# Gate and value products of four column tiles as seven block products, in a chain of attention and two feed-forwards

## The chip, the cores and the metric

One core of one Trainium2 chip runs the whole kernel. The metric is the device time of an execution in microseconds (us): 484.2 us before the change, the median of 3 runs (484.12 to 484.35). Engines: TensorE (PE in the profile, PEld its weight loads), VectorE (DVE), ScalarE (ACT), GpSimd (POOL) and SyncE (SP), which issues the DMAs here.

## The reference, cut to what matters

Attention over 2 x 12 heads, 448 tokens and 64 columns with capped scores, then two feed-forwards over the 896 tokens. The change is in the second one, and in five small instructions at the start:

```
scores = cap * tanh(scale * q @ k.T / cap)          # attention, 12 heads x 2
x  = moe(x, w_in, w_out, g_ln)                      # first feed-forward: 896 x 768 out
g  = x @ w_gate                                     # 896x768 @ 768x1536
silu = g * (1 / (1 + exp(-g)))
val  = x @ w_val                                    # 896x768 @ 768x1536
out  = (silu * val) @ w_out                         # 896x1536 @ 1536x768
```

The weights arrive as 64-bit floats and are brought to 32 bits on the chip.

## The kernel before, in words

Every 32-bit operand of a product is split into a high and a low part (`split`, L627: the high part is a ScalarE copy, the low part a VectorE subtraction), and `mm3` (L175) issues three matmuls for one product: high by high, high by low, low by high. Accumulators are PSUM tiles of one bank; eight banks are handed round under the tag `m`.

The stage of gate and value (loop at L947) goes over `K2` = 12 column tiles `fc` of 128 columns (the third to sixth are `fc` 2 to 5, called tile 2 to tile 5 here), and in each over the tokens in two blocks, 384 and 512. `ff2_gv` (L603) makes `g` and then `v` for a block: 6 row tiles of `x2` times three matmuls, so 18 matmuls for one accumulator. ScalarE takes the Silu of `g` into `ee`, VectorE multiplies by `v`, forms sums for the output stage (`S1f`, `S3f`) and splits the result into `a`. So a column tile is 72 matmuls, 36 of 384 and 36 of 512 tokens.

`load_gv` (L593) brings the weights of tile `fc + 1` while tile `fc` runs: one DMA of 766 KB into one of two `raw` buffers, `f32_shifted` (L158: two ScalarE passes and one VectorE pass into one of two `f32` buffers), and a split into `g4`, of which there are four, two for even and two for odd tiles. `load_w2` (L632) does the same for a tile of the output weights; L954 calls it once in each of tiles 2 to 8.

The matrix `x2` (tokens after the first feed-forward, transposed) is made just before by `ff1_x2` (L570): each block of 24 matmuls is drained as a ScalarE copy (high) and a VectorE subtraction (low). At the same time `load_w_out` (L558) makes the next weights with both engines.

The order is set by a scheduler within this stage (`in_order` off): it places instructions by its own model of their times, under the waits that the tiles require. Each engine then runs its own list strictly in that order, and an instruction that waits holds up all behind it.

In `setup` (L190), L201 to L206 convert -9 * 2^30 to a 32-bit integer and back, and add what it differs from -2^31 to `cap`; `c1`, the scale of the first tanh, is made from that.

Of the kernel before, what the change touches and what calls it, by code (L numbers as in the profile page):

```python
# [37 lines left out]
class Kernel:  # L38
# [135 lines left out]

    def mm3(self, out, lhsT, rhs, start, stop):  # L175

        mm = self.PE.matmul
        mm(out, lhsT[0], rhs[0], start=start, stop=False)
        mm(out, lhsT[0], rhs[1], start=False, stop=False)
        mm(out, lhsT[1], rhs[0], start=False, stop=stop)  # L180

# [8 lines left out]
    def setup(self):  # L190
# [9 lines left out]
        nc.gpsimd.dma_start(cp, self.cap.to_broadcast([128, 1]))  # L200
        low, least = cs[:, 6:7], cs[:, 7:8]  # L201
        self.G.memset(low, -9.0 * 2.0 ** 30)
        self.A.activation(least.bitcast(I32), low, AF.Copy)
        self.V.tensor_copy(low, least.bitcast(I32))
        self.V.tensor_scalar(low, low, 2.0 ** 31, None, op0=ALU.add)
        self.V.tensor_tensor(cp, cp, low, op=ALU.add)  # L206
        self.V.reciprocal(c1, cp)
# [362 lines left out]
    def ff1_x2(self, j, get, N, o):  # L570
# [3 lines left out]
        def part(a, z):  # L574
            def f():
# [17 lines left out]
    def load_gv(self, fc, i):  # L593

        if i == 0:
            self.gvs[fc] = [self.g4[(fc % 2) * 2 + n].rearrange("p (u k f) -> p u k f", u=2, f=128) for n in range(2)]
# [6 lines left out]
    def ff2_gv(self, fc, N, o):  # L603
# [236 lines left out]
    def run(self):  # L840
# [69 lines left out]
        self.g4 = [p.tile([128, 1536], F32R, name=f"g4_{i}", tag=f"g4_{i}") for i, p in enumerate((wb, wb, gb, gb))]  # L910
        w8 = self.w8 = wb.tile([128, 8, 2, n], F32R, name="w8", tag="w8")
        X = self.slot("x", [128, KD, 2, 896], "x2")
# [19 lines left out]
        big = self.big = self.slot("l", [128, 6144], "a_0")  # L932
        self.A12t, self.A22t = (ap.tile([128, KD, 2, w], F32R, name=f"a_{i}", tag=f"a_{i}") for i, w in ((1, n), (2, 512)))
        self.S1f, self.S3f = (ap.tile([128, KD, n], F32, name=f"s_{i}", tag=f"s_{i}") for i in (1, 3))
        w1 = ap.tile([128, 2, n], F32R, name="w1", tag="w1")
        t1 = ap.tile([128, n], F32, name="t1", tag="t1")
# [64 lines left out]
```

## Time and profile before

| | before |
|---|---|
| median of 3 runs | 484.20 us |
| the profiled execution's own time | 485.15 us |
| its span in the profile | 483.4 us |
| PE busy | 478.9 us, 99% of the span |
| DVE busy | 337.8 us, 70% |
| ACT busy | 290.3 us, 60% |
| POOL busy | 20.9 us, 4% |
| granted TensorE clock | 1.00 of full speed, 2.4 GHz |

The span is what the profiler saw of the engines; the own time of the same execution is 1.75 us more, and lies 0.95 us over the median of the runs. Matmuls are pipelined: the mean of a matmul's record is longer than the distance from one to the next, which is read from the chain of waits or from busy time over count. Idle time of an engine that nobody waits for costs nothing.

### The profile page before, as it was taken

What the parts mean: (1) busy time and instruction counts of PE and PEld (TensorE: products, weight loads), DVE (VectorE), ACT (ScalarE), POOL (GpSimd) and SP (SyncE); (2) the same over time, 40 slices, a digit from 0 to 9 for tenths busy, and PEclk for the clock granted to TensorE, in tenths of its full rate; (3) what the DMA queues carried; (4) which work ended last, traced back from release to release, by engine and by line L of the source; (5) the groups of instructions that cost most, each with busy time, mean ns of one, the idle gap of its engine ahead of it and who ended that gap; (6) DMA issues with size and microseconds to landing.
All of it is one profiled execution on the core that took longest, in us unless ns stands there. A gap on an engine that the chain in (4) does not pass through costs nothing.

```text
span 483.4 us, 7642 instructions
## 1 busy us (share of the span) xinstructions
PE 478.9 (99%) x3042; PEld 394.7 (82%) x3042; DVE 337.8 (70%) x577; ACT 290.3 (60%) x407; POOL 20.9 (4%) x63
## 2 busy tenths in 40 slices
PE   9999999999999999999999999999999999999997
PEld 7444444538888899989899988899988899999996
DVE  3689999987769987475546454556554427999991
ACT  5999999931233796457857766667764416335220
POOL 1020101021000010000000000000000000000000
PEclk9999999999999999999999999999999999999999
DMA  6886575002001323236663454654462401010012
GB/s 176 202 190 153 146 185 146 20 2 87 0 1 41 90 75 101 83 113 194 196 196 109 152 187 139 196 184 134 137 194 68 131 0 57 11 60 7 18 54 94
DMA packets 65060, 52.35 MB, mean 108 GB/s; under 512 B 35584, under 2 KB 61952, under 8 KB 64256
## 3 DMA queue, kind: packets, MB, share of 16 engines
q1 hardware_dynamic: 64992, 51.86, 36.0%
q8 instruction: 24, 0.39, 0.3%
q14 instruction: 12, 0.10, 0.1%
q0 software_dynamic: 32, 0.00, 0.0%
HBM read 49.10 MB, written 2.75 MB: 107 GB/s over the span
## 4 chain that ended last, share of the span: by engine, by line
PE 99%; DVE 1%; issue 0%
PE g L30 18%; PE v L30 18%; PE p L30 16%; PE x L30 12%; PE h L30 12%; PE pv L30 8%; PE sc L30 7%; PE S L30 4%; PE lt L30 1%; PE T L30 1%; PE warm L30 1%; DVE ks L30 0%; PE T_q L30 0%; PE warm_T L30 0%; DVE ee L30 0%; PE T_k L30 0%
## 5 line engine op out<-in xcount | busy, mean ns | idle before, releaser
L30 PE MATMUL g<-x,g 128*128 128x512 f32 (+1 forms) x432 | 91.7, 363 | 0.0
L30 PE MATMUL v<-x,g 128*128 128x512 f32 (+1 forms) x432 | 90.8, 362 | 0.0
L30 PEld LDWEIGHTS g<-x,g 128*128 128x128 f32 x432 | 78.5, 188 | 8.9
L30 PEld LDWEIGHTS v<-x,g 128*128 128x128 f32 x432 | 78.2, 188 | 8.6
L30 PE MATMUL h<-wi,x 128*128 128x512 f32 x252 | 59.1, 392 | 0.0
L30 PEld LDWEIGHTS h<-wi,x 128*128 128x128 f32 x252 | 46.8, 188 | 11.2 <-issue 1.5
L30 ACT ACTIVATE P<-sc,consts 112x896 f32<-112x896 f32 x48 | 45.3, 1009 | 3.8 <-PE sc L30 2.2
L30 ACT ACTIVATE P<-P,consts 112x3584 f32<-112x3584 f32 (+1 forms) x13 | 39.7, 3061 | 0.1
L30 PE MATMUL pv<-P,v 112*32 112x448 f32 x384 | 38.5, 540 | 0.0
L30 PEld LDWEIGHTS sc<-ks 64*112 64x112 f32 x288 | 23.3, 171 | 18.3 <-issue 7.7
L30 PE MATMUL sc<-ks 64*112 64x448 f32 x288 | 35.8, 379 | 0.3
L30 PE MATMUL x<-lB,wo 128*128 128x256 f32 (+1 forms) x192 | 35.2, 337 | 0.0
L30 PEld LDWEIGHTS x<-lB,wo 128*128 128x128 f32 x192 | 29.6, 189 | 3.4
L30 PEld LDWEIGHTS pv<-P,v 112*32 112x32 f32 x384 | 12.2, 110 | 23.0 <-issue 20.9
L30 ACT ACTIVATE ee<-h,sms 128x512 f32<-128x512 f32 x14 | 9.5, 683 | 33.2 <-DVE sms L30 33.2
L30 DVE TENSOR_TENSOR g<-wg,g 128x768 fp32r<-128x768 f32 x12 | 11.5, 959 | 25.2 <-ACT g L30 25.2
L30 PE MATMUL x<-lA,wo 128*128 128x384 f32 x144 | 27.4, 338 | 0.0
L30 PE MATMUL p<-w,a 128*128 128x384 f32 x144 | 26.7, 334 | 0.0
L30 PEld LDWEIGHTS x<-lA,wo 128*128 128x128 f32 x144 | 25.2, 188 | 0.5
L30 DVE TENSOR_TENSOR ee<-v,ee 128x384 f32<-128x384 f32 (+2 forms) x24 | 12.5, 520 | 18.5 <-PE v L30 17.7
L30 PEld LDWEIGHTS p<-w,a 128*128 128x128 f32 x144 | 25.2, 188 | 0.1
L30 ACT ACTIVATE g<-wg 128x768 fp32r<-128x768 f32 x12 | 10.1, 846 | 24.0 <-PE g L30 23.3
(178 smaller groups left out, 737.5 us busy)
## 6 DMA issues: line engine op xcount, KB each, us to landing
wg_raw<-in_moe_w_gate_dram SPq DMA_DIRECT2D x12, 765.8 KB, 4.3
wv_raw<-in_moe_w_val_dram SPq DMA_DIRECT2D x12, 765.8 KB, 4.2
wi_raw<-in_moe_w_in_dram SPq DMA_DIRECT2D x6, 1024.0 KB, 6.8
wo_raw<-in_moe_w_out_dram SPq DMA_DIRECT2D x12, 512.0 KB, 3.5
w_raw<-in_moe_w_out_dram SPq DMA_DIRECT2D x6, 767.6 KB, 4.3
v<-in_v_dram SPq DMA_DIRECT2D x24, 112.0 KB, 3.8
kq<-in_k_dram SPq DMA_DIRECT2D x22, 112.0 KB, 2.8
kq<-in_q_dram SPq DMA_DIRECT2D x22, 112.0 KB, 2.7
```

The lines of the kernel that those rows point to most:

```text
L30: i = f(*a, **k)
```

## The change: what it does

For tiles 2 to 5 the products of gate and value are formed together as a 2 x 2 block product: rows gate and value of the weights, their 768 rows in halves of 384, and the tokens in halves of 448. Seven products of sums of blocks (Strassen's scheme in Winograd's form) take the place of eight: each is 3 row tiles times 3 matmuls of 448 tokens, so 63 matmuls for a tile. The sums have to be made:

- of `x2`, once: `ff1_x2` also copies each accumulator to `xf` in 32 bits (one more ScalarE instruction for each of 14 blocks), and `x_sums` makes four differences of 384 x 448 (three row tiles of 448, 1344 elements a partition) and splits them into `T1` to `T4`, in tiles 0 and 1.
- of the weights, for each tile: `sum_steps(fc + 1)` loads and converts both, two sums of 384 elements go to GpSimd (`S`), two to VectorE, and the splits go to `g4[0]` (A11, A12), `g4[1]` or `g4[3]` (S2, S4), `g4[2]` (S3, S1) and `w1` (A22). Only the second of these is double-buffered.
- of the results: accumulators `a` (named `g_` in the rows), `b` and `c` are each used twice: a first product is read out, then a second is added to it in the same bank. `ee` holds `sg`, `c22`, `p1` and `u2` once.

`xf` takes the room of `w8`, so the loads of the output weights move from tiles 2 to 8 to tiles 6 to 9, two in each of tiles 6 to 8. `load_gv` takes tile 6 as before. The conversion at the start (L201 to L206) is left out.

```diff
-        low, least = cs[:, 6:7], cs[:, 7:8]
-        self.G.memset(low, -9.0 * 2.0 ** 30)
-        self.A.activation(least.bitcast(I32), low, AF.Copy)
-        self.V.tensor_copy(low, least.bitcast(I32))
-        self.V.tensor_scalar(low, low, 2.0 ** 31, None, op0=ALU.add)
-        self.V.tensor_tensor(cp, cp, low, op=ALU.add)
...
                     self.hi_act(hi, ps)
                     self.lo_dve(lo, ps, hi)
+                    self.A.activation(self.xf[:, j, o:o + N], ps, AF.Copy)
...
+    def x_sums(self, i):
+        x = [self.xf[:, 3 * (m // 2):3 * (m // 2) + 3, 448 * (m % 2):448 * (m % 2) + 448] for m in range(4)]
+        d, p, m, t = ((0, 1, 0, 0), (1, 3, 1, 2), (3, 3, 0, 1), (2, 2, 3, 3))[i]
+        self.V.tensor_tensor(x[d], x[p], x[m], op=ALU.subtract)
+        self.split([self.T[t][:, u] for u in range(2)], x[d])
+    def sum_steps(self, fc):
+        add, sub = ALU.add, ALU.subtract
+        f = []
+        for n, w in zip("gv", (self.w_gate, self.w_val)):
+            src = w[:, fc * 128:(fc + 1) * 128].rearrange("(k p) f -> p k f", p=128)
+            f.append(self.f32_shifted(self.load_shifted(src, f"w{n}_{fc}"), f"w{n}_{fc}").rearrange("p (h x) -> p h x", h=2))
+        g, v = f
+        s1 = self.t1
+        pair = lambda t: [t.rearrange("p (h u x) -> p h u x", h=2, u=2)[:, :, u] for u in range(2)]
+        t = self.gvs[fc] = [self.g4[0], self.g4[1 + fc % 2 * 2], self.g4[2], self.w1]
+        S = self.G
+        S.tensor_tensor(s1, v[:, 0], v[:, 1], op=add)
+        S.tensor_tensor(v[:, 0], g[:, 0], v[:, 0], op=sub)
+        def first():
+            self.split(pair(t[0]), g)
+            self.V.tensor_tensor(g[:, 0], s1, g[:, 0], op=sub)
+            self.V.tensor_tensor(g[:, 1], g[:, 1], g[:, 0], op=sub)
+            self.split(pair(t[1]), g)
+        def second():
+            hi, lo = pair(t[2])
+            for m, x in enumerate((v[:, 0], s1)):
+                self.split((hi[:, m], lo[:, m]), x)
+        def third():
+            self.split([self.w1[:, u] for u in range(2)], v[:, 1])
+        return first, second, third
+    def ff2_gv_seven(self, fc):
+        V, add, mult = self.V, ALU.add, ALU.mult
+        n, k, ee = self.HN, fc, self.ee
+        a, s24, s31, a22 = self.gvs[fc]
+        half = lambda t, h: t.rearrange("p (h u k f) -> p h u k f", h=2, u=2, k=3)[:, h]
+        A11, A12, S2, S4, S3, S1 = (half(t, h) for t in (a, s24, s31) for h in range(2))
+        A22 = a22.rearrange("p u (k f) -> p u k f", k=3)
+        X = lambda kh, th: [[self.x2[3 * kh + c][:, u, 448 * th:448 * th + 448] for u in range(2)] for c in range(3)]
+        T1, T2, T3, T4 = ([[t[:, u, c] for u in range(2)] for c in range(3)] for t in self.T)
+        bank = lambda m: self.pt.tile([128, 512], F32, name=f"{m}_{fc}", tag="m")[:, :448]
+        def product(acc, w, x, start):
+            for c in range(3):
+                self.mm3(acc, (w[:, 0, c], w[:, 1, c]), x[c], start and c == 0, c == 2, not start)
+        sg, c22, p1, u2 = (ee[:, 448 * m:448 * m + 448] for m in range(4))
+        last = fc + 1 == self.KD
+        first, second, third = (lambda: None,) * 3 if last else self.sum_steps(fc + 1)
+        if last:
+            self.load_gv(fc + 1, 1)
+        a = bank("g")
+        product(a, A11, X(0, 0), True)
+        self.A.activation(p1, a, AF.Copy)
+        b = bank("b")
+        product(b, S2, T2, True)
+        V.tensor_tensor(u2, p1, b, op=add)
+        product(a, A12, X(1, 0), False)
+        self.A.activation(sg, a, AF.Silu)
+        first()
+        if last:
+            self.load_gv(fc + 1, 0)
+        product(b, S3, T3, False)
+        V.tensor_tensor(p1, p1, b, op=add)
+        c = bank("c")
+        product(c, S1, T1, True)
+        V.tensor_tensor(c22, p1, c, op=add)
+        second()
+        e = bank("e")
+        product(e, A22, T4, True)
+        V.tensor_tensor(p1, p1, e, op=add)
+        third()
+        product(c, S4, X(1, 1), False)
+        V.tensor_tensor(u2, u2, c, op=add)
+        self.A.activation(u2, u2, AF.Silu)
+        V.tensor_tensor(p1[:, :n], p1[:, :n], sg[:, :n], op=mult)
+        V.tensor_tensor(self.S1f[:, k, :64], p1[:, n:], sg[:, n:], op=mult)
+        self.split(self.A11[k], p1[:, :n])
+        V.tensor_tensor(self.S1f[:, k, 64:], c22[:, :320], u2[:, :320], op=mult)
+        V.tensor_tensor(c22[:, 320:], c22[:, 320:], u2[:, 320:], op=mult)
+        V.tensor_tensor(self.S3f[:, k], p1[:, :n], self.S1f[:, k], op=ALU.subtract)
+        self.split(self.A61[k], c22[:, 320:])
...
-        w8 = self.w8 = wb.tile([128, 8, 2, n], F32R, name="w8", tag="w8")
+        self.xf = wb.tile([128, 6144], F32, name="xf", tag="w8")[:, :KD * 896].rearrange("p (k n) -> p k n", k=KD)
...
-        self.A12t, self.A22t = (ap.tile([128, KD, 2, w], F32R, name=f"a_{i}", tag=f"a_{i}") for i, w in ((1, n), (2, 512)))
+        a12 = ap.tile([128, KD * 2 * 896], F32R, name="a_1", tag="a_1")
+        self.T = [a12[:, 2688 * i:2688 * i + 2688].rearrange("p (u k n) -> p u k n", u=2, k=3) for i in range(4)]
+        self.A12t, self.A22t = (a12[:, KD * 2 * a:KD * 2 * z].rearrange("p (k u n) -> p k u n", k=KD, u=2)
+                                for a, z in ((0, n), (n, 896)))
...
+        early = {6: (6, 8), 7: (0, 1), 8: (2, 3), 9: (4,)}
         for fc in range(K2):
+            if 2 <= fc < KD:
+                self.ff2_gv_seven(fc)
+                continue
+            if fc == KD:
+                w8 = self.w8 = wb.tile([128, 8, 2, n], F32R, name="w8", tag="w8")
+                w = both(w8) + [(w1[:, 0], w1[:, 1])]
+                w += [p for g in self.g4[:2] for p in both(g.rearrange("p (k u n) -> p k u n", k=2, u=2))]
+                self.B11, self.B21 = w[4:10], w[:4] + w[10:12]
             for i, (N, o) in enumerate(((n, 0), (512, n))):
-                if fc + 1 < K2:
+                if fc == 1:
+                    if i == 0:
+                        first, second, third = self.sum_steps(2)
+                        first()
+                elif fc + 1 < K2:
                     self.load_gv(fc + 1, i)
                 elif i == 0:
                     self.load_w2(5)
                     self.load_w2(10)
-                if i == 1 and 2 <= fc < 9:
-                    self.load_w2((6, 8, 0, 1, 2, 3, 4)[fc - 2])
+                for c in early.get(fc, ())[i:i + 1]:
+                    self.load_w2(c)
                 self.ff2_gv(fc, N, o)
+                if fc < 2:
+                    self.x_sums(2 * fc + i)
+            if fc == 1:
+                second()
+                third()
```

TensorE, tiles 2 and 3 before: `g` and `v` with the tile's number, 18 matmuls each.

```order
L30 MATMUL g_2_0_2701<-x2_1938,g4_0_1933 128x384 x18
L30 MATMUL v_2_0_2720<-x2_1938,g4_1_1934 128x384 x18
L30 MATMUL g_2_384_2761<-x2_1938,g4_0_1933 128x512 x18
L30 MATMUL v_2_384_2780<-x2_1938,g4_1_1934 128x512 x18
L30 MATMUL g_3_0_2813<-x2_1938,g4_2_1935 128x384 x18
L30 MATMUL v_3_0_2832<-x2_1938,g4_3_1936 128x384 x18
L30 MATMUL g_3_384_2873<-x2_1938,g4_2_1935 128x512 x18
L30 MATMUL v_3_384_2892<-x2_1938,g4_3_1936 128x512 x18
```

The same place now, from the second use of `b` of tile 2 on (`g_3` is the accumulator `a` of tile 3; `g4_0` holds A11 and A12, `g4_2` S3 and S1, `a_1` the sums of `x2`):

```order
L30 MATMUL b_2_2748<-a_1_2492,g4_2_1930 128x448 x9
L30 MATMUL e_2_2800<-a_1_2492,w1_2495 128x448 x3
L30 MATMUL g_3_2847<-x2_1933,g4_0_1928 128x448 x9
L30 MATMUL b_3_2858<-a_1_2492,g4_3_1931 128x448 x2
L30 MATMUL c_3_2895<-a_1_2492,g4_2_1930 128x448 x9
L30 MATMUL e_3_2910<-a_1_2492,w1_2495 128x448 x7
L30 MATMUL c_2_2785<-x2_1933,g4_1_1929 128x448 x9
L30 MATMUL b_3_2858<-a_1_2492,g4_3_1931 128x448 x7
L30 MATMUL e_3_2910<-a_1_2492,w1_2495 128x448 x2
L30 MATMUL g_3_2847<-x2_1933,g4_0_1928 128x448 x9
L30 MATMUL b_3_2858<-a_1_2492,g4_2_1930 128x448 x9
```

Products of 9 take the place of 18; the scheduler has moved the last product into `c_2` behind three products of tile 3, and cut some products in two. The last row but one is the second use of `g_3` (A12), right behind the first products of `b`, `c` and `e` of tile 3.

ScalarE, tile 3 before (`wg_5`, `wv_5` are the gate and value weights of tile 5 being converted; `ee<-g` is the Silu):

```order
L30 ACTIVATE wg_5_2919<-wg_5_raw_2917,consts_106 128x768 [waits DMAHW0_49,DVE_49]
L30 ACTIVATE ee_174<-g_3_0_2813 128x384 [waits DVE_49,PE_49]
L30 ACTIVATE wg_5_2919<-wg_5_2919,consts_106 128x768 [waits Activation_49]
L30 ACTIVATE wv_5_2969<-wv_5_raw_2967,consts_106 128x768 [waits DMAHW1_49,DVE_49]
L30 ACTIVATE wv_5_2969<-wv_5_2969,consts_106 128x768 [waits Activation_49]
L30 ACTIVATE a_0_2482<-ee_174 128x384 [waits DVE_49]
L30 ACTIVATE g4_2_1935<-wg_5_2919 128x768 [waits PE_49]
L30 ACTIVATE ee_174<-g_3_384_2873 128x512 [waits PE_49]
L30 ACTIVATE w2_0_2977<-w2_0_raw_2975,consts_106 128x768 [waits DMAHW2_49,DVE_49]
L30 ACTIVATE w2_0_2977<-w2_0_2977,consts_106 128x768 [waits Activation_49]
L30 ACTIVATE g4_3_1936<-wv_5_2969 128x768 [waits PE_49]
L30 ACTIVATE w8_1937<-w2_0_2977 128x384 [waits DVE_49]
```

ScalarE now, from the conversion of tile 4's weights to the copy of `p1` of tile 3 (last row); `ee<-ee` of 448 is the Silu of `u2` of tile 2, and `g4_2<-t1` is the high part of S1, a sum that GpSimd makes:

```order
L30 ACTIVATE wg_4_2835<-wg_4_raw_2833,consts_106 128x768 [waits DMAHW4_49,DVE_49]
L30 ACTIVATE wg_4_2835<-wg_4_2835,consts_106 128x768 [waits Activation_49]
L30 ACTIVATE wv_4_2841<-wv_4_raw_2839,consts_106 128x768 [waits DMAHW5_49,DVE_49]
L30 ACTIVATE a_0_2491<-ee_169 128x384 [waits DVE_49]
L30 ACTIVATE wv_4_2841<-wv_4_2841,consts_106 128x768 [waits Activation_49]
L30 ACTIVATE g4_2_1930<-t1_2496 128x384 [waits PE_49,Pool_49]
L30 ACTIVATE ee_169<-ee_169 128x448 [waits DVE_49]
L30 ACTIVATE w1_2495<-wv_4_2841 128x384 [waits PE_49]
L30 ACTIVATE a_0_2491<-ee_169 128x128 [waits DVE_49]
L30 ACTIVATE ee_169<-g_3_2847 128x448 [waits DVE_49,Activation_49]
```

The copy that frees `g_3` for its second product now stands behind both weights' conversion for the next tile, behind a row that waits for GpSimd, and behind the Silu of the tile before.

## Rows read from the trace of the kernel before

**Rows 1.** The page, busy time (share) and instructions by engine

```profile
PE 478.9 (99%) x3042; PEld 394.7 (82%) x3042; DVE 337.8 (70%) x577; ACT 290.3 (60%) x407; POOL 20.9 (4%) x63
```

**Rows 2.** Chain that ended last, the third column tile: start us, us, what

```profile
257.24 3.14 PE g L30 x18
260.38 3.12 PE v L30 x18
263.50 4.12 PE g L30 x18
267.62 4.08 PE v L30 x18
```

**Rows 3.** Tiles 2 and 5: us; busy us (x) PE, PEld, DVE, ACT, POOL; clock

```profile
257.24:271.70 14.46, 14.46 (x73) 13.02 (x73) 7.97 (x14) 9.94 (x15) 0.00 (x0) 1.00 0.50 163
...
300.64:315.10 14.46, 14.46 (x73) 13.02 (x73) 7.99 (x14) 9.51 (x14) 0.00 (x0) 1.00 0.51 164
```

**Rows 4.** Groups of instructions, whole span: busy us, mean ns | idle before

```profile
L30 PE MATMUL x<-lB,wo 128*128 128x256 f32 x96 | 12.0, 282 | 0.0
...
L30 DVE SCALAR_TENSOR_TENSOR wg<-wg_raw,wg 128x768 uint32<-128x768 uint32 x12 | 11.5, 958 | 9.8 <-ACT wg L30 9.8
...
L30 DVE TENSOR_TENSOR g<-wg,g 128x768 fp32r<-128x768 f32 x12 | 11.5, 959 | 25.2 <-ACT g L30 25.2
...
L30 DVE TENSOR_TENSOR x<-pv,tr 128x448 f32<-128x448 f32 x12 | 7.5, 624 | 1.2
...
L30 DVE TENSOR_TENSOR a<-ee,a 128x384 fp32r<-128x384 f32 x12 | 6.6, 554 | 3.1 <-ACT a L30 3.1
...
L30 DVE TENSOR_TENSOR ee<-v,ee 128x128 f32<-128x128 f32 x6 | 1.7, 280 | 0.0
...
L30 ACT ACTIVATE wg<-wg_raw,consts 128x768 f32<-128x768 int8 x12 | 12.0, 998 | 6.1 <-DVE g L30 4.1 <-DMA wg_raw<-in_moe_w_gate_dram 2.0
...
L30 ACT ACTIVATE wg<-wg,consts 128x768 int32<-128x768 f32 x12 | 11.2, 932 | 0.1
...
L30 ACT ACTIVATE g<-wg 128x768 fp32r<-128x768 f32 x12 | 10.1, 846 | 24.0 <-PE g L30 23.3 <-DVE wg L30 0.7
...
L30 ACT ACTIVATE a<-ee 128x384 fp32r<-128x384 f32 x12 | 6.3, 524 | 10.0 <-DVE ee L30 9.5
...
L30 ACT ACTIVATE ee<-g 128x512 f32<-128x512 f32 x12 | 7.0, 584 | 4.3 <-PE g L30 4.3
...
L30 POOL TENSOR_TENSOR sms<-sms,consts 128x1 f32<-128x1 f32 x7 | 4.5, 641 | 64.1 <-DVE sms L30 64.1
```

**Rows 5.** Timeline around the third column tile's start: start us, us, engine, instruction

```profile
255.85 0.94 ACT L30 ACTIVATE w<-w,consts 128x768 int32<-128x768 f32 x1
...
256.82 0.96 DVE L30 SCALAR_TENSOR_TENSOR w<-w_raw,w 128x768 uint32<-128x768 uint32 x1 [2.02 <-ACT w L30]
...
257.70 0.55 DVE L30 TENSOR_TENSOR s<-v,ee 128x384 f32<-128x384 f32 x1
257.81 0.37 SPq L155 DMA_DIRECT2D wv_raw<-in_moe_w_val_dram  x1
...
262.06 1.00 ACT L30 ACTIVATE wv<-wv_raw,consts 128x768 f32<-128x768 int8 x1 [0.33 <-DMA wv_raw<-in_moe_w_val_dram]
```

**Rows 6.** Timeline of the stage that makes x2, its fifth block

```profile
199.61 0.67 ACT L30 ACTIVATE wo<-wo_raw 128x512 f32<-128x512 f32 x1
199.75 0.69 DVE L30 TENSOR_TENSOR x<-x,x 128x512 fp32r<-128x512 f32 x1 [1.66 <-ACT x L30]
...
212.34 0.68 DVE L30 TENSOR_TENSOR wo<-wo,wo 128x512 fp32r<-128x512 f32 x1
...
213.52 2.27 PE L30 MATMUL x<-lA,wo 128*128 128x384 f32 x12
```

**Rows 7.** Timeline of the start

```profile
4.34 0.16 DVE L30 TENSOR_TENSOR consts<-consts 128x1 f32<-128x1 f32 x1 [1.65 <-DMA consts<-in_cap_dram]
...
8.70 3.70 ACT L30 ACTIVATE P<-sc,consts 112x896 f32<-112x896 f32 x4 [0.73 <-PE sc L30]
```

More of the change, by code (lines that the diff above doesn't have):

```diff
@@ L173, in transpose, with mm3 @@
         self.PE.matmul(out, src, ident, is_transpose=True)
-    def mm3(self, out, lhsT, rhs, start, stop):
+    def mm3(self, out, lhsT, rhs, start, stop, more=False):
         mm = self.PE.matmul
-        mm(out, lhsT[0], rhs[0], start=start, stop=False)
-        mm(out, lhsT[0], rhs[1], start=False, stop=False)
-        mm(out, lhsT[1], rhs[0], start=False, stop=stop)
+        kw = {"skip_group_check": True} if more else {}
+        mm(out, lhsT[0], rhs[0], start=start, stop=False, **kw)
+        mm(out, lhsT[0], rhs[1], start=False, stop=False, **kw)
+        mm(out, lhsT[1], rhs[0], start=False, stop=stop, **kw)
     def pool(self, name, bufs=1, side="left", space=None):
@@ L593, in load_gv @@
     def load_gv(self, fc, i):
-        if i == 0:
+        if fc not in self.gvs:
             self.gvs[fc] = [self.g4[(fc % 2) * 2 + n].rearrange("p (u k f) -> p u k f", u=2, f=128) for n in range(2)]
@@ L932, in run @@
         big = self.big = self.slot("l", [128, 6144], "a_0")
-        self.A12t, self.A22t = (ap.tile([128, KD, 2, w], F32R, name=f"a_{i}", tag=f"a_{i}") for i, w in ((1, n), (2, 512)))
+        a12 = ap.tile([128, KD * 2 * 896], F32R, name="a_1", tag="a_1")
+        self.T = [a12[:, 2688 * i:2688 * i + 2688].rearrange("p (u k n) -> p u k n", u=2, k=3) for i in range(4)]
+        self.A12t, self.A22t = (a12[:, KD * 2 * a:KD * 2 * z].rearrange("p (k u n) -> p k u n", k=KD, u=2)
+                                for a, z in ((0, n), (n, 896)))
         self.S1f, self.S3f = (ap.tile([128, KD, n], F32, name=f"s_{i}", tag=f"s_{i}") for i in (1, 3))
-        w1 = ap.tile([128, 2, n], F32R, name="w1", tag="w1")
+        w1 = self.w1 = ap.tile([128, 2, n], F32R, name="w1", tag="w1")
         t1 = ap.tile([128, n], F32, name="t1", tag="t1")
@@ L943, in run @@
         self.T1f = [self.ee[:, n + 512 + n * i:n + 512 + n * (i + 1)] for i in range(3)] + [t1, self.sms]
-        w = both(w8) + [(w1[:, 0], w1[:, 1])]
-        w += [p for g in self.g4[:2] for p in both(g.rearrange("p (k u n) -> p k u n", k=2, u=2))]
-        self.B11, self.B21 = w[4:10], w[:4] + w[10:12]
+        self.t1 = t1
+        early = {6: (6, 8), 7: (0, 1), 8: (2, 3), 9: (4,)}
         for fc in range(K2):
-            for i, (N, o) in enumerate(((n, 0), (512, n))):
-                if fc + 1 < K2:
+            if 2 <= fc < KD:
[6 more added lines that the diff above has]
+                self.B11, self.B21 = w[4:10], w[:4] + w[10:12]
+            for i, (N, o) in enumerate(((n, 0), (512, n))):
+                if fc == 1:
[3 more added lines that the diff above has]
+                elif fc + 1 < K2:
                     self.load_gv(fc + 1, i)
```

## The prediction

> **What bounds the kernel now.** I read the page's busy shares first: TensorE is busy 99% of the span and no other engine over 70% [rows 1]. The chain of waits says the same of the stage that changes: it is nothing but `g` and `v` matmuls back to back. A block of 384 tokens takes 3.14 and 3.12 us for 18 matmuls, 174 ns each; one of 512 takes 4.12 and 4.08 us, 228 ns each; the four make 14.46 us, one column tile [rows 2]. The view by stretches shows what lies beside it: in tiles 2 and 5 VectorE is busy 8.0 us and ScalarE 9.5 to 9.9 us of 14.46, GpSimd not at all, and the clock is 1.00, the level of 2.4 GHz [rows 3]. So fewer or shorter matmuls shorten the kernel one for one, as long as the 6.5 us of slack on VectorE and the 4.5 us on ScalarE are not used up.
>
> **The change part by part.**
>
> *Matmuls.* Between 384 and 512 tokens the pitch rises by 54 ns for 128 tokens, 0.42 ns a token, with 12 ns that don't depend on the tokens. The matmuls of 256 tokens lie on that line: 12.0 us for 96 is 125 ns [rows 4], the line gives 120. For 448 tokens it gives 201 ns; the rows on both sides, 174 and 228, are the ends. 63 of them are 12.66 us instead of 14.46: 1.80 us a tile, 7.2 us for four. With the ends it would be 14.0 and 0.4 us. I take 7.2.
>
> *VectorE's load in tiles 2 to 4.* Two passes of the conversion at 0.958, two low parts of 768 at 0.959, eight instructions of 384 at 0.554, five sums of 448 that read PSUM at 0.624, two of 128 at 0.28 [rows 4], and the product of `S1f` in two pieces of 64 and 320, 0.7 together by interpolation: 1.92 + 1.92 + 4.43 + 3.12 + 0.56 + 0.70 = 12.6 us in 21 instructions. TensorE's tile is 12.66. An instruction that waits for nothing new starts 0.08 us before the end of the one in front (256.82 + 0.96 against 257.70), and one that waits for another engine starts 0.03 after it (255.85 + 0.94 against 256.82) [rows 5]; so the list takes 11.3 to 12.6 us, and its idle time has next to no room. ScalarE adds up to 9.7 us: four conversion passes 3.86, two high parts of 768 1.69, four of 384 2.10, three of 448 at most 1.75, one of 128 about 0.3 [rows 4]. Neither engine is over the limit by its sum. What decides is the round trip in the lists, which I walk with these durations and hand-offs.
>
> *The round trip in tile 3.* Accumulator `a` can't take its second product before ScalarE has copied it to `p1`, and `p1` is free only when tile 2 is finished on VectorE. Time 0 is tile 2's first matmul. 41 matmuls later, at 8.2, the second product of tile 2's `a` is done, and only then may `g4[0]` be rewritten: high part 0.85, low part 0.96. Then VectorE has the sum for S2 (0.55), `p1 + b` (0.62), the low part of S3 (0.55), the other sum (0.55) and the low part for `w1` (0.55), which frees the `f32` buffer: 12.6. ScalarE ends the high part of S2 at 13.0, then converts tile 4's gate and value weights (3.86) with a high part (0.52) between: 17.2. VectorE ends the value weights (0.96): 18.2. GpSimd adds their halves: no row shows it. Its bounds are the same instruction on VectorE (0.55) and that plus GpSimd's own 0.64 for one element [rows 4], 1.2; I take 0.9, the middle: 19.1. ScalarE then makes the high part of S1 (0.52) and the Silu of `u2` (0.58): 20.3; VectorE 0.48, 0.28, 0.55 and 0.55 up to `S3f`: 22.0; ScalarE the copy of `p1`: 22.5. TensorE stands before that product after 99 matmuls, at 19.9. It waits 2.6 us, 2.2 to 2.9 with GpSimd's ends.
>
> [...]
>
> *Tiles 4 and 5.* The last product of `c` waits until VectorE has read the first: after the second product of `b` come `p1 + b`, a sum, a low part and `c22`, 0.62 + 0.55 + 0.55 + 0.62 less the overlaps and with the hand-offs, 2.2 us, against 1.81 of TensorE's work on the next `a`: 0.4 us, for tile 3 and tile 4. Behind it the first product of the next `b` needs the high part of S2: that comes 4.4 us after the same moment (the buffer at 1.6, two passes 1.94, the high part 0.85), TensorE is there at 4.0: 0.4 us, twice. In tile 5 the copy of `p1` stands on ScalarE behind the conversion of tile 7's gate weights. Its DMA goes when VectorE has ended tile 6's value weights, at 44.4 if the walk is continued with the same durations; issue to use is 4.25 us [rows 5], then 1.0, 0.3 and 0.54: 50.4, and TensorE is there at 49.4: 1.0 us. In tile 6 nothing is late by this walk.
>
> *The stage of x2.* The extra copies are 14 ScalarE instructions of at most 0.58 [rows 4], some 7 us; ScalarE is not the limit there, but each waits for VectorE's low part and holds the list. Before, the absolute value of `w_out`'s fifth block started at 199.61, beside VectorE's low part from 199.75 to 200.44; now the copy comes after that and in front of it, and VectorE takes an `x_sums` difference of 1344 elements, some 1.5 us, in front of the block's next passes. The low part of the block's second half was ready at 212.34 + 0.68 = 213.02 and is read by the third matmul from 213.52 on, 213.87 [rows 6]: 0.85 us of margin against 2.1 in front. The ends are 0 (all of it falls in VectorE's own waits) and 1.3; I take 0.5. In tiles 0 and 1 VectorE gets four differences and four low parts of 1344, 12.4 us by the 1.05 ns an element between 384 and 768, beside some 6.6 a tile of its own and 1.1 of sums: 26.7 of 28.9. That just fits, so 0.
>
> *Moves at no cost.* The loads of the output weights: tiles 6 to 8 carry one more than in rows 3, which is 3.0 us of ScalarE and 2.1 of VectorE, so 12.9 and 10.1 of 14.46, and the next tile's weights have a whole tile of lead; without that cover each late load would cost its 4 us. SyncE issues the same DMAs in the changed order, none of them past another that TensorE waits for except the one counted in tile 5. The check at the start: the reciprocal waits for the DMA of `cap`, not for the five instructions (VectorE waited 1.65 us for it), and `c1` is used only from 8.70 [rows 7], 4 us later: 0.
>
> *Sum.* -7.2 + 2.6 + 0.8 + 0.8 + 1.0 + 0.5 = -1.5 us; with GpSimd's page rate -1.6. That is against the profiled execution, 485.15 us, span 483.4: 483.65 and 481.9. It lies 0.95 over the median, so 484.2 - 1.5 = 482.7 us for the median.
>
> **The rivals.**
>
> *The waits are hidden.* The scheduler cut and reordered products so that they would be; if the hand-offs come out shorter than walked, or PSUM is seen as ready before the matmul's modelled end, most of the 5.7 us go. For it: TensorE waits for nothing in this stage before [rows 2]. Against it: each wait is a sum of durations that the rows show. Time: between 484.2 - 7.2 = 477.0 and 480.5.
>
> *VectorE paces the tiles (slower).* If its instructions don't overlap in this order, a tile takes the whole 12.6, 21 hand-offs at 0.03, 0.6, and the idle time that the walk has in it, 0.7 us for the rewritten `g4[0]` and 1.0 behind the second product of `b`: 14.9. From 14.46 on nothing of the saving is left. Tiles 2 to 4 then cost 1.3 us more than before, tile 5 with its lighter list saves 1.8 less 1.0, x2 costs 0.5: 485.2; with tile 3's wait of 2.6 on top, since then nothing absorbs it, 487.8. The middle is 486.5. For it: nearly every instruction of the list waits for another engine or for the one in front. Against it: the overlap in rows 5.
>
> *The clock falls.* The longest gap of TensorE is 2.6 us by the walk. In this trace it is idle 4.5 us in all, start and end included [rows 1], and the clock of the stage is 1.00 [rows 3], so no row shows what such a gap does. At 1.2 GHz a product of 1.81 would take 1.81 more; two of them behind the gap, 3.6: 486.3. [...]
>
> *The change doesn't do what it says.* The order of the changed kernel has 63 matmuls of 448 for each of the four tiles, so I give that nothing.
>
> **How the numbers follow.** A measurement of this kernel can tell some 0.2% from no change, 1.0 us: faster is under 483.2, slower over 485.2. My forecast, part of the saving kept (481.0 to 485.0): 0.50, of it 0.33 faster and 0.17 the same. Waits hidden: 0.20, faster. VectorE paces: 0.20, slower but for 0.03 the same. The clock: 0.05, slower. The rest, 0.05, is split between 448 tokens at another pitch (0.02 faster) and some stall elsewhere (0.03 the same). Faster 0.55, the same 0.23, slower 0.22. The range goes from 479.0, which leaves out half of the case of hidden waits, to 486.2, which leaves out the worse half of VectorE's; the forecast's own is 481.0 to 485.0.
>
> **What would show it.** In the profile after: 448-token matmuls at about 201 ns by the chain; VectorE busy 12 us or more of each of tiles 2 to 4; TensorE idle once, 2 to 3 us, before the second product of `g_3`, ended by ScalarE's copy of `p1`, with GpSimd's sum in the chain behind it; smaller gaps before the last `c` and the next `b`; one near the end of tile 5 that leads back to a DMA of `wg`; tile 6 on at 14.46. It would be wrong if TensorE ran through tile 3 without a gap, or if VectorE had no idle time there at all.

## The result: 491.3 us, 1.4% slower, and the profile after

The changed kernel takes 491.32 us (median of 4 runs, 490.53 to 492.51) against 484.27; the ratio is 1.0144 with an interval of 1.0122 to 1.0165. The prediction was 482.7, between 479.0 and 486.2: wrong in sign and outside the range. The profiled execution took 491.82 us with a span of 490.1, 6.7 longer than that of before.

The page of after, busy time by engine and the clock in 40 slices, answers to [rows 1]:

```profile
PE 477.1 (97%) x3006; PEld 391.3 (80%) x3006; DVE 371.3 (76%) x626; ACT 305.0 (62%) x440; POOL 30.9 (6%) x70
...
PEclk9999999999999998999999989999999999999999
```

TensorE is busy only 1.8 us less, and two slices have an 8 where all were 9. The view by stretches, first of before, then of after, at the same places in the program: PE's first matmul of x2 to the third block row of `w_out`, from there to tile 2, tiles 2 to 6, tiles 7 to 11 (of after the second stretch is cut at 192). Columns as in [rows 3].

```profile
167.77:183.61 15.84, 15.84 (x113) 15.81 (x113) 13.50 (x35) 15.62 (x37) 1.46 (x2) 1.00 0.21 67
183.61:257.24 73.63, 73.63 (x386) 66.66 (x385) 43.25 (x71) 48.22 (x87) 0.00 (x0) 1.00 0.45 143
257.24:329.57 72.33, 72.33 (x361) 65.11 (x361) 39.86 (x66) 48.69 (x68) 0.00 (x0) 1.00 0.51 164
329.57:401.90 72.33, 72.33 (x361) 65.11 (x361) 33.31 (x50) 35.95 (x50) 0.00 (x0) 1.00 0.35 109
```

```profile
167.80:187.27 19.47, 16.46 (x115) 15.87 (x114) 14.61 (x36) 17.32 (x43) 1.14 (x2) 1.00 0.18 56
187.27:192.00 4.73, 4.73 (x22) 4.73 (x23) 3.98 (x9) 2.67 (x7) 0.00 (x0) 0.64 0.17 42
192.00:262.95 70.95, 70.70 (x364) 63.23 (x363) 49.40 (x70) 50.57 (x90) 4.34 (x2) 1.00 0.39 123
262.95:336.22 73.27, 69.25 (x325) 61.14 (x325) 55.32 (x97) 47.57 (x73) 6.09 (x6) 0.98 0.42 131
336.22:408.56 72.34, 72.34 (x362) 65.13 (x361) 40.72 (x60) 45.05 (x63) 0.00 (x0) 1.00 0.52 162
```

The stage of x2 has grown by 3.63 us up to the third block row and by 2.05 behind it (4.73 + 70.95 against 73.63): 5.7. Tiles 2 to 6 take 0.94 more, tiles 7 to 11 what they took. Together that is 6.6 of the 6.7 us. What TensorE waits for in after (of before the list has only 0.8 us at the start and nothing later):

```profile
PE x L30 <- ACT wo L30: 2.9, 1, 2.9
PE g L30 <- ACT ee L30: 2.9, 2, 2.1
...
PE c L30 <- DVE ee L30: 0.7, 2, 0.4
...
```

Two more are of 0.3. The other rows, of 0.8, 0.7 and 0.5 us, lie in the first 18 us; the x2 stage still begins at 167.80 us against 167.77.

**The stage of x2.** The first wait lies in the stage that I had priced at 0.5. ScalarE's timeline of before, then of after, shows the list that leads to the high part of the third `w_out` block (`wo` 128x512 to fp32r; `xf` are the new copies):

```profile
175.14 0.66 ACT L30 ACTIVATE wo<-wo_raw 128x512 f32<-128x512 f32 x1
...
178.68 1.28 ACT L30 ACTIVATE wo<-wo,gt 128x128 f32<-128x128 f32 x4
...
181.43 0.62 ACT L30 ACTIVATE wo<-wo 128x512 fp32r<-128x512 f32 x1
```

```profile
177.44 0.38 ACT L30 ACTIVATE xf<-x 128x256 f32<-128x256 f32 x1
177.70 0.67 ACT L30 ACTIVATE wo<-wo_raw 128x512 f32<-128x512 f32 x1
...
182.81 0.39 ACT L30 ACTIVATE x<-x 128x256 fp32r<-128x256 f32 x1 [1.95 <-PE x L30]
183.09 0.48 ACT L30 ACTIVATE xf<-x 128x384 f32<-128x384 f32 x1
183.46 0.60 ACT L30 ACTIVATE lB<-lt 128x512 fp32r<-128x512 f32 x1
183.94 1.28 ACT L30 ACTIVATE wo<-wo,gt 128x128 f32<-128x128 f32 x4
...
185.84 0.65 ACT L30 ACTIVATE wo<-wo 128x512 fp32r<-128x512 f32 x1
```

The block's first pass starts 2.6 us later, its scaling stands behind `x`, a copy and `lB`, and its high part comes at 185.84 instead of 181.43, 4.4 later. TensorE had 1.5 us of room (182.05 against 183.61) and waits the rest, 2.9. Then the clock falls: 0.64 over 187.27 to 192.00, the only place in the stage.

No copy waits for VectorE here. The low parts that the copies at 177.44 and 183.09 had to follow were over at 176.08 and 181.67:

```profile
175.66 0.42 DVE L30 TENSOR_TENSOR x<-x,x 128x256 fp32r<-128x256 f32 x1 [0.40 <-ACT x L30]
...
181.12 0.55 DVE L30 TENSOR_TENSOR x<-x,x 128x384 fp32r<-128x384 f32 x1
```

From 168 us to the late high part ScalarE's only wait is the 1.95 us for TensorE, in front of the high part of `x` at 182.81. Before, that instruction came behind the scaling and the high part of the block; now it stands in front of both. So what the copies changed here is the order that the scheduler makes of the list. Of the 3.7 us from 182.81 to the end of the block's high part in the chain of waits, 0.65 are the copies' own time.

**Tile 3.** The chain of waits, up to the second product of `g_3`:

```profile
283.28 0.43 PE e L30 x2
...
284.13 0.51 DVE w L30
284.64 0.48 DVE s L30
...
285.20 0.55 ACT ee L30
...
285.80 2.78 PE g L30 x9
288.57 2.72 PE b L30 x9
...
298.17 1.82 PE e L30 x9
```

That is the predicted wait at the predicted instruction (`s` is `S3f`, `ee` the copy of `p1`), and the two products behind it take 2.78 and 2.72 us instead of 1.82.

### The profile page after: what moved, and what is told of

It reads as the page before. It is cut to its first block, busy times and chain, and to the rows that moved or that the text cites. A ratio compares the mean times of both kernels' runs of the same rounds, so it can differ in the third digit from the quotient of the medians.

```text
span 490.1 us, 7688 instructions
## 1 busy us (share of the span) xinstructions
PE 477.1 (97%) x3006; PEld 391.3 (80%) x3006; DVE 371.3 (76%) x626; ACT 305.0 (62%) x440; POOL 30.9 (6%) x70
## 4 chain that ended last, share of the span: by engine, by line
PE 91%; DVE 3%; DMA 2%; ACT 2%; issue 1%; SPq 1%; DVEq 0%; ACTq 0%
PE p L30 16%; PE g L30 14%; PE h L30 12%; PE v L30 12%; PE x L30 11%; PE pv L30 7%; PE sc L30 6%; PE S L30 4%; PE b L30 3%; PE c L30 2%; DMA kq<-in_q_dram 1%; PE lt L30 1%; DVE wo L30 1%; PE e L30 1%; PE T L30 1%; DMA wg_raw<-in_moe_w_gate_dram 1%
## 5 line engine op out<-in xcount | busy, mean ns | idle before, releaser
L30 PE MATMUL g<-x,g 128*128 128x384 f32 (+2 forms) x360 | 78.5, 367 | 2.9 <-ACT ee L30 2.9
L30 PEld LDWEIGHTS g<-x,g 128*128 128x128 f32 x360 | 66.1, 189 | 10.7 <-ACT ee L30 3.6
L30 PE MATMUL v<-x,g 128*128 128x512 f32 (+1 forms) x288 | 60.9, 362 | 0.0
L30 PEld LDWEIGHTS v<-x,g 128*128 128x128 f32 x288 | 52.2, 188 | 5.8
L30 PE MATMUL x<-lA,wo 128*128 128x384 f32 x144 | 29.0, 349 | 3.3 <-ACT wo L30 2.9
L30 DVE TENSOR_TENSOR x<-x,x 128x448 fp32r<-128x448 f32 (+3 forms) x26 | 15.3, 587 | 10.5 <-ACT x L30 10.0
L30 DVE TENSOR_TENSOR g<-wg,g 128x768 fp32r<-128x768 f32 x16 | 15.3, 955 | 9.5 <-ACT g L30 8.8
L30 PE MATMUL S<-P,ones 112*32 112x448 f32 x192 | 22.4, 549 | 0.0
```

Of the source, the lines that this page charges most:

```text
L30: i = f(*a, **k)
```

## The experiments

Theory 1: the copies of x2 make a block late in ScalarE's list, TensorE waits, and its clock falls behind the wait. Theory 2: the same in tile 3, by the single `p1`. Rivals: the sums on VectorE, the scheduler's order, GpSimd's sums, the check. Ratios are to the runs of before that shared the chip; differences in us are of medians, each first taken against those runs (the changed kernel: +7.1), so the two can differ by some 0.2%.

**The copies alone.** The loop's `ff2_gv_seven`, `sum_steps` and `x_sums` are taken out:

```diff
-            if 2 <= fc < KD:
-                self.ff2_gv_seven(fc)
-                continue
...
```

> The changed kernel with all twelve column tiles on the old products of 384 and 512 tokens: of the change only ScalarE's copies of x2 (written, read by nothing), the late loads of the output weights and the missing end check are left. Theory 1 (the copies fill ScalarE's list in the x2 stage, the high part of a w_out block comes late, TensorE waits 2.9 us for it and its clock then falls): the stage of x2 is 5.7 us longer than before, the gap of about 2.9 us near 184 is there, and the total is 484.3 + 5.7 = 490.0, 489.0 to 491.0. Rival (it is the sums of x2 on VectorE, or the order that the scheduler chose because of them, that make the stage longer): 484.3 to 485.5 and no gap over 0.5 us there.

490.33 us, ratio 1.0123 (1.0088 to 1.0158): 5.5 us slower than before, without one product by seven. The wait is there, 2.9 us for `wo`, and ScalarE's list has the same order as in after. So the copies alone make the whole loss of the x2 stage; the rival (the sums of x2, or an order made for them) falls.

**The wait kept, TensorE kept busy.**

```diff
-        steps += wo[3] + x2[2][0][:1] + x2[0][2] + x2[1][2]
+        warm = lambda: self.keep_warm(30, self.pt.tile([128, 512], F32, name="warm_x2", tag="m"))
+        steps += wo[3] + [(0.0, warm)] + x2[2][0][:1] + x2[0][2] + x2[1][2]
```

> The changed kernel with 30 small matmuls of constants in front of the matmul that waits 2.9 us for ScalarE in the stage of x2; the wait itself stays. If the fall of the clock behind that gap costs time of its own, the clock stays at 1.00 from 187 to 192 and the total is 491.3 - 1.9 = 489.4 (489.0 to 489.9). Rival (behind the gap it is ScalarE's and VectorE's chain through the w_out blocks that sets the time, and a faster TensorE only waits later): 491.3, with waits of some 2 us that turn up behind 190.

488.99 us, ratio 1.0094 (1.0074 to 1.0114): +4.2, so 2.9 less than the changed kernel. TensorE's timeline:

```profile
183.28 3.71 PE L30 MATMUL warm_x<-const-float32-1.0 128*64 128x64 f32 x60
186.92 2.35 PE L30 MATMUL x<-lA,wo 128*128 128x384 f32 x12
...
284.26 2.09 PE L30 MATMUL g<-x,g 128*128 128x448 f32 x9 [2.10 <-ACT ee L30]
286.19 1.98 PE L30 MATMUL b<-a,g 128*128 128x448 f32 x9
```

The block starts as late as in after, but at the full clock (1.00 over 187 to 192 us), and from there to tile 2 it takes 74.41 us instead of 75.68: the fall of the clock had a price of 1.3 us of its own. Unexpected: in tile 3 the same pause of 2.10 us is followed by products at full speed here (granted clock 1.00 over 284 to 294 us). Of the four runs two have a mean clock of 1.000 (488.52 and 488.58 us), two of 0.997 (489.40 and 490.04). That fits a pause that lowers the clock in some executions and not in others; only the profiled run shows the place, so this is not shown.

**A second buffer for `p1`.**

```diff
+        if fc % 2:
+            p1 = self.xfb[:, 5376:5824]
...
```

> The changed kernel with a second buffer for p1 in tiles 3 and 5 (in the memory of x2's f32 form behind what is used), so that the copy of the first product doesn't wait for the end of the tile before. Theory 2 (the wait before the second product of g_3 is the single p1, and the clock falls because of that gap): the gap of 2.1 us and the two slow products behind it go, 491.3 - 2.1 - 1.9 = 487.3 (486.8 to 488.3). Rival (the round trip is set as well by the rewriting of g4_0 and GpSimd's sums, so that TensorE waits at the next product instead): a gap of 1 to 2 us remains in tile 3, 489.5 to 491.3.

485.49 us, ratio 1.0013 (1.0004 to 1.0023): +0.7, 6.4 less than the changed kernel. The wait and the slow products of tile 3 are gone:

```profile
282.95 1.99 PE L30 MATMUL g<-x,g 128*128 128x448 f32 x9
...
285.40 2.10 PE L30 MATMUL b<-a,g 128*128 128x448 f32 x9
```

Tile 5's wait is gone too, and the waits of `c` and `b` in tile 4; tiles 2 to 6 go from 73.27 to 67.13 us. The x2 stage keeps its 2.9. Theory 2 holds. I expected 4.0 because I had left out tile 5 (1.1) and tile 4 (0.9).

**The f32 form of x2 by GpSimd.**

```diff
-                    self.A.activation(self.xf[:, j, o:o + N], ps, AF.Copy)
+                    self.G.tensor_tensor(self.xf[:, j, o:o + N], hi.bitcast(F32), lo.bitcast(F32), op=ALU.add)
```

> The changed kernel, with the f32 form of x2 made by GpSimd as the sum of high and low part, instead of by ScalarE's 14 copies out of PSUM. Theory 1: the gap of 2.9 us and the fall of the clock near 184 to 192 go, the stage of x2 takes what it took before, total 491.3 - 5.7 = 485.6 (485.0 to 486.6). Rival (the order of the stage, not the copies): still 491. Second rival (GpSimd's adds slow VectorE's instructions beside them): part of it comes back, 487 to 489, with VectorE's low parts longer than 0.69 us.

482.46 us, ratio 0.9958 (0.9944 to 0.9972): -2.4. The wait near 184 is gone and the clock is 1.00 there. A wait of 1.4 us remains at 215, now for the low part of the fifth block, which is where I had looked for the loss. VectorE's timeline there, and before:

```profile
200.11 1.84 DVE L30 TENSOR_SCALAR wo<-wo 128x512 f32<-128x512 f32 x2
200.27 1.40 POOL L30 TENSOR_TENSOR xf<-x 128x512 f32<-128x512 f32 x1 [1.56 <-DVE x L30]
```

```profile
200.36 0.88 DVE L30 TENSOR_SCALAR wo<-wo 128x512 f32<-128x512 f32 x2
```

The same pair takes 1.84 us beside a GpSimd addition and 0.88 without. That alone does not make the block late: with the same additions and VectorE's differences of x2 held back (below) the pair still takes 1.84 us, and the wait at 215 is gone. More came back than the 5.7 of the stage: tile 3 has no wait in this kernel although `p1` is single, and the scheduler now puts the last product of tile 2 earlier, as in the next run.

**One line moved: the copy in front of the low part.**

```diff
                     self.hi_act(hi, ps)
+                    self.A.activation(self.xf[:, j, o:o + N], ps, AF.Copy)
                     self.lo_dve(lo, ps, hi)
-                    self.A.activation(self.xf[:, j, o:o + N], ps, AF.Copy)
```

> The changed kernel with each of ScalarE's copies of x2 put directly behind the high part and in front of VectorE's low part, so that the copy waits for nothing and the low part waits for it. If the loss in the x2 stage comes from the copies' waits for VectorE in ScalarE's list, the gap near 184 falls under 1.5 us, the clock holds and the time is 486 to 488. Rival (the copies' own 0.4 to 0.6 us each, in a list that is already full, make the w_out block late): a gap of 2.5 us or more, 490.5 to 492.

481.81 us, ratio 0.9925 (0.9899 to 0.9950): -2.8, 9.9 less than the changed kernel with the same instructions, and below the 486 to 488 expected, since tile 3's loss goes too. The rival (the copies' time) is out as the cause of the loss. ScalarE's list and what TensorE waits for behind the start:

```profile
179.35 1.28 ACT L30 ACTIVATE wo<-wo,gt 128x128 f32<-128x128 f32 x4
...
182.41 0.62 ACT L30 ACTIVATE wo<-wo 128x512 fp32r<-128x512 f32 x1
```

```profile
PE c L30 <- DVE ee L30: 0.7, 2, 0.4
PE g L30 <- ACT ee L30: 0.6, 1, 0.6
```

The high part comes at 182.41, in time. From PE's first matmul of x2 to tile 2 it takes 0.5 us more than before. In tile 3 there is no wait: the last product of `c_2` stands right behind the first of `g_3` (from 268.58), not behind three products more:

```profile
270.40 1.99 PE L30 MATMUL c<-x,g 128*128 128x448 f32 x9
```

So the place of one copy decides both losses, and both by the order that the scheduler makes: in the x2 stage the scaling is back in front of the high part of `x` that waits for TensorE. Why the scheduler puts it behind when the copy follows the low part is not shown; it goes by its own model of the times.

**No copies; copies in front alone.** In the first run the copies are taken out and the sums are made of the high parts alone; the second is the run of the copies alone with the line moved.

```diff
...
-        self.V.tensor_tensor(x[d], x[p], x[m], op=ALU.subtract)
+        self.V.tensor_tensor(x[d], h[p], h[m] if i < 2 else x[m], op=ALU.subtract)
...
```

> The changed kernel without ScalarE's copies of x2: the sums for the seven products are made of the high parts alone (the low part of x2 is left out of the sums; the instructions on VectorE and TensorE are the same). If the copies cost only by their waits and by the order that follows from them: as with the copies in front, 481.8 (481.2 to 482.2), without a gap near 184. If the copies' own time on ScalarE has a price: 0.5 us or more faster than that, 481.3 or less. Rival (VectorE's sums in the stage of x2 hold it up by themselves): a gap of more than 1 us in that stage, 483 or more.

> All twelve tiles on the old products, and the copies of x2 (read by nothing) in front of the low parts. If the copies behind the low parts cost 5.5 us by their waits, the same copies in front cost next to nothing: 484.3 to 485.2, no gap near 184, clock 1.00. Rival (the products by seven change the scheduler's order, and that is what took the loss away): 488 or more.

481.11 us, ratio 0.9926 (0.9912 to 0.9941), and 485.05, 1.0009 (0.9999 to 1.0018). With the old products the copies in front cost 0.5 us by the medians, with an interval that includes nothing, against 5.5 behind the low parts; ScalarE's list there is that of before with the copies set in (scaling at 178.41, high part at 181.48). The late loads and the missing check are in this run too, so they cost no more than that. Beside the seven products the copies cost nothing that the intervals can tell (0.9925 with, 0.9926 without); by the medians the kernel without them is 0.6 us faster (-3.4 against -2.8), and 481.11 lies in the range of my second case (a price of their own), so a small one is not excluded.

**GpSimd's sums on VectorE.** `S = self.V` instead of `self.G`.

> The changed kernel with the two sums of weight halves of each tile on VectorE instead of GpSimd. If GpSimd's sums (about 1 us each) lengthen the round trip of tile 3, the gap before the second product of g_3 shrinks from 2.1 to some 1.6 us and the time to 490.0 to 491.0. Rival (VectorE paces the tiles): two more instructions of 0.55 us a tile on VectorE make the gap longer or add waits, 492 or more. If neither is on the path that ends last: 491.3, within 0.5.

488.78 us, ratio 1.0070 (1.0046 to 1.0093): +4.1, 2.9 less than the changed kernel, where I had expected some 1 us. Tile 3's pause:

```profile
284.54 2.09 PE L30 MATMUL g<-x,g 128*128 128x448 f32 x9 [1.53 <-ACT ee L30]
```

1.53 us instead of 2.10, and the product behind it takes 2.09 instead of 2.78: the clock holds (1.00 over 284 to 289 us). Tiles 2 to 6 take 70.91 us instead of 73.27: GpSimd was on the path for 0.6, and the clock made 2.4 of it. VectorE doesn't pace the tiles.

**Both repairs; sums held back; two and three edits.** The first combines GpSimd's additions with two buffers for `p1`, the second adds program order for `x_sums`; the others start from the moved line.

> Both repairs at once: the f32 form of x2 made by GpSimd, and the second buffer for p1 in tiles 3 and 5. If the two losses are separate places, the stage of x2 is as with the first repair alone (1.8 us longer than before the change) and tiles 2 to 5 as with the second alone (5.2 us shorter than before the change): 484.3 - 3.4 = 480.9 (480.2 to 481.7). Rival (the first repair already took tile 3's wait away, and the second adds nothing): as the first repair alone, 482.0 to 482.5.

> Both repairs, and VectorE's differences of x2 held back until tiles 0 to 2, so that none of them stands in the stage of x2. If the difference of 1344 elements (1.55 us near 202.6) is what makes the low part of the fifth w_out block late, the remaining gap of 1.4 us near 215 goes: 1.4 us faster than both repairs alone, about 479.5. Rival (VectorE's instructions take longer beside GpSimd's additions, and that makes the block late): at most 0.4 us better. Second rival: VectorE is now overloaded in tiles 1 and 2, and TensorE waits there for a sum of x2: 481 or more.

> The copies in front of the low parts, and the second buffer for p1 in tiles 3 and 5. What is left of waits in tiles 2 to 5 with the first edit alone are 0.36, 0.36 and 0.60 us, each with some 0.3 us for a product that starts anew; if the single p1 is behind the last of them, 481.8 - 0.9 = 480.9. Rival (the scheduler's new order puts another wait in its place, as it did with GpSimd's sums and two buffers, 1.6 us for the high part of S2): 481.8 to 482.8.

> The copies in front of the low parts, and the sums of weight halves on VectorE instead of GpSimd. If GpSimd's sums are still on the path in tiles 3 to 5: about 0.5 us faster than the first edit alone, 481.3. Rival (they are hidden now, and VectorE has room): 481.8, within 0.4. Second rival (VectorE's list becomes the bound): 483 or more.

> All three edits: the copies in front, two buffers for p1, the sums on VectorE. If each takes away a wait of its own, 481.8 - 0.9 - 0.5 = 480.4 (479.8 to 481.0). Rival (one wait stands behind another, set by the order that the scheduler makes of it): 481.5 to 482.5.

482.54 (0.9943), 482.20 (0.9945), 481.00 (0.9922), 482.30 (0.9944) and 480.96 us (0.9917, 0.9898 to 0.9936). The gains don't add. With two buffers a wait of 1.6 us for the high part of S2 takes the place of the other: GpSimd's additions with two buffers miss the 480.9 that I expected and come out near the rival, while the moved line with two buffers has the rival's wait and still the time that I expected without it. With the sums held back the wait at 215 goes, and one of 1.9 us in tile 2 for a sum of x2 takes its place, the rival, not the 479.5 expected. VectorE's sums on top of the moved line gave none of the 0.5 expected. With all three no wait behind the start is over 0.54 us, and the time lies in the range expected. By their intervals none is told apart from the moved line alone.

**The check put back** into the form with two edits.

> The copies in front and two buffers for p1, with the check at the start put back (five instructions in front of the reciprocal). If the check lies beside the wait for the DMA and ahead of any use of its result, the time is that without it, 481.0 within 0.4. Rival (the five instructions delay the first Tanh): up to 1 us slower, 481.5 to 482.0.

481.12 us, ratio 0.9925 (0.9909 to 0.9942) against 0.9922: nothing, as predicted.

**What a pause costs.** The kernel before, with pauses in front of tiles 7 to 11:

```diff
+    def gap(self, fc, k):
...
+        self.PE.matmul(a, self.z, self.z, start=True, stop=True)
+        self.A.activation(d[:64, :64], a, AF.Copy)
+        for _ in range(k):
+            self.G.tensor_copy(d[:, :16], d[:, :16])
+        self.PE.matmul(b, d[:, :64], d[:, :64], start=True, stop=True)
...
+            if fc >= 7:
+                self.pinned = nc.tensor
+                self.gap(fc, (1, 3, 5, 7, 9)[fc - 7])
```

> The kernel before, with a pause of TensorE in front of tiles 7 to 11, made by a chain of one copy on ScalarE and 1, 3, 5, 7 and 9 small copies on GpSimd: about 1.0, 1.7, 2.3, 3.0 and 3.6 us by 0.3 us a copy. It tells what a pause costs beside itself in a stream that is otherwise without gaps. If the clock falls behind pauses of some 2 us and more, tiles 9, 10 and 11 begin with 2 us of matmuls at the lower clock, tile 7 doesn't: 484.3 + 11.6 + 6 = 502, 499 to 505. Rival (a pause costs only itself, and the clock fell for another reason): 484.3 + 11.6 = 496, clock 1.00 behind all of them. Second rival (any pause lowers the clock): 506.

517.06 us, ratio 1.0656, outside the 499 to 505 expected. The pauses came out longer than meant (ScalarE's copy stood behind its list), so this doesn't tell where the fall begins, and the second rival (any pause lowers the clock) is not tested by it. Two of the five, and what follows:

```profile
332.53 0.33 PE L30 MATMUL gap<-consts 128*64 128x64 f32 x2 [2.33 <-POOL consts L30]
332.79 4.98 PE L30 MATMUL g<-x,g 128*128 128x384 f32 x18
...
416.26 0.48 PE L30 MATMUL gap<-consts 128*64 128x64 f32 x2 [4.34 <-POOL consts L30]
416.67 6.03 PE L30 MATMUL g<-x,g 128*128 128x384 f32 x18
```

Undisturbed, 18 such matmuls take 3.14 us [rows 2] by the chain and some 3.3 by such a row. After each of the five pauses, 2.33 to 5.11 us, the clock fell, to a mean of 0.50 to 0.68 of full speed over the next 3.6 to 4.9 us, for 1.5 to 2.7 us of price beside the pause. The rival that a pause costs only itself is out.

## Why the prediction was wrong

| step | predicted, us | measured in after |
|---|---|---|
| matmuls | -7.2 | -6.9 (1.82 / 9 = 202 ns; 63 are 12.74) |
| wait of tile 3 | +2.6 | +2.1, and 0.4 in front of it |
| the clock behind it | 0 (rival, 0.05) | +1.9 |
| waits of `c` and `b` | +0.8 + 0.8 | +1.8 |
| tile 5 | +1.0 | +1.1 |
| x2 stage | +0.5 | +5.7 |
| check, tiles 7 to 11 | 0 | 0 |

With a rest of 0.5 in tiles 2 to 6 that is 6.6 of the 6.7 us that the span grew. The 0.4 in front is the first `b` of tile 3. Tile 3's wait and clock are read from the chain above (285.80 - 283.71; 2.77 and 2.73 to the next start, less 1.82 each), the other waits from the starts in TensorE's timeline:

```profile
291.12 2.02 PE L30 MATMUL g<-x,g 128*128 128x448 f32 x9
293.47 2.09 PE L30 MATMUL c<-x,g 128*128 128x448 f32 x9 [0.32 <-DVE ee L30]
295.67 0.67 PE L30 MATMUL b<-a,g 128*128 128x448 f32 x2
...
313.59 1.58 PE L30 MATMUL b<-a,g 128*128 128x448 f32 x7
315.93 2.13 PE L30 MATMUL g<-x,g 128*128 128x448 f32 x9 [0.75 <-ACT ee L30]
```

From `g` to `c` 2.35 and from `c` to `b` 2.20 instead of 1.82 make 0.9, and again in tile 4; 2.34 instead of 1.42 is tile 5's. A wait that the row gives as 0.32 us costs 0.53 from start to start.

*The step that failed is the x2 stage.* I wrote that each copy "waits for VectorE's low part and holds the list", took the list otherwise in the order of before, and priced the stage at 0.5 by one block, the fifth, whose margin I had read. At that block 0.5 us was lost: TensorE goes on at 219.50 us after two matmuls that began at 218.63, 0.87 instead of 0.35. The loss stands two blocks earlier. From 167.77 to 183.61 ScalarE is busy 15.62 of 15.84 us before the change, in a row that the prediction doesn't use, and the third block had only 1.5 us of room. There the scheduler put the block's passes behind others, TensorE waited 2.9 us, and the clock fell for 1.3 more; the remaining 1.0 of the 5.7 is not taken apart. That the loss is the copies' place and the order that follows from it, not in the main their own time, is shown by the moved line; that it is not a copy held up by VectorE is shown by the rows above. The prediction walked the changed lists in tiles 3 to 5 and not in this stage.

Later in the stage copies do wait as I wrote, up to 0.76 us at 205.56 and at 215.29 us. The copy and the low part read the same PSUM tile on two engines; in after each of the 14 copies begins only when the low part of its block has ended, four of them after a wait of 0.49 to 0.76 us for it. Why the pair is put in order is not shown.

*The second failed step is the clock.* I found the pause of 2.6 us and its price if the clock fell, and gave it 0.05 because no row of before shows a pause. It fell twice, to 0.64 of full speed over 4.7 us behind 2.9 us of idle time and to 0.66 over 5.0 us behind 2.1, and cost 1.3 and 1.9 us. That it is TensorE's idle time that the fall follows is shown by the run with TensorE kept busy: the same wait for ScalarE left the clock at 1.00 from 187 to 192 us. Nothing in the rows of before let me expect the fall behind pauses as short as these. The price, two products at half of full speed, 3.6 us, was an assumption with no row of before behind it; in after the clock was 0.50 over 188 to 190 and over 288 to 290 us, and the two products behind tile 3's wait took 1.9 us more. Full speed as 2.4 GHz is an estimate: [rows 2] give one token in 0.42 ns, 2.4 a ns.

No run shows the rate for GpSimd that the -1.6 beside the sum uses. In after its additions of 384 elements took 1.01 or 1.02 us in seven of eight, where the -1.5 has 0.9.

*Right were* the pitch of 448 tokens, the walk through tiles 3 to 5 with each wait at its instruction, and the check. VectorE was less busy than I had said, 29.4 of the 42.05 us from 262.95 to 305.00, where 12 us or more in each tile were to be a sign. Of the rivals, VectorE pacing did not happen: TensorE waits at single hand-offs and runs at 1.82 a product between them. The forecast comes near the kernel with the moved line, which has neither of the two failures: x2 +0.5, tiles 2 to 6 -3.6 us, in all -2.8 by the medians where -1.5 was predicted; there tile 3's wait of 2.6, a term of the sum, is missing too, so the nearness is in part luck.

## What to carry to other kernels

An instruction added to an engine's list is priced where that list is fullest, and by the order that comes of it, not by its own time alone: look for the stretch in which the engine is busy all the time, read the changed list there, and see what now stands behind an instruction that waits. Here it was enough to put the new one where its input was ready. Tile 3's pause of 2.1 us cost 4.0, nearly twice its length, when the clock fell behind it, so a small saving on the path to it can return more than itself (0.6 us by VectorE's sums returned 2.4). And where a scheduler orders the lists, a repair moves waits that have nothing to do with it: measure the pair, don't add the gains.

## What was not expected of the hardware

- The clock fell behind pauses of 2.1 us (after, to 0.66 of full speed over 5.0 us), 2.9 (to 0.64 over 4.7) and all five of 2.33 to 5.11 (to 0.50 to 0.68); behind 2.1 us in tile 3 of the kernel with TensorE kept busy it held at 1.00 in the profiled run, and so it did behind six pauses of 1.36 to 1.88 us in the profiled runs of five others. In two of the nine runs of the kernel with the pause of 1.88 the mean clock was 0.996.
- How low it was behind a pause, and for how long, differs. In the kernel with five pauses the first 16 matmuls behind 2.33 us took 3.71 us at 0.62, and behind 4.34 us 4.93 at 0.50:

```profile
332.79:336.50 3.71, 3.71 (x16) 3.71 (x15) 2.13 (x4) 2.80 (x4) 0.00 (x0) 0.62 0.58 169
...
416.67:421.60 4.93, 4.93 (x16) 4.93 (x16) 0.00 (x0) 0.00 (x0) 0.00 (x0) 0.50 0.00 0
```

- Two VectorE instructions of one input took 1.84 us together beside a GpSimd addition of 1.40, and 1.98 beside one of 1.67, instead of 0.88. The cause is not shown.
- GpSimd's addition of 384 elements of the weights took 1.01 or 1.02 us seven times in after, where I had taken 0.9, and once 3.33, before tile 2; in the kernel in which it also made x2 the two groups of four took 1.22 and 1.37 on average.
